# Second layer of a two-layer expert kernel: another order of the seven products, sums formed one step earlier, token operands in nine steps

## The chip, the core and the metric

The kernel runs on one core of a Trainium2 chip. A core has engines with a program each: TensorE (PE, matrix products), VectorE (DVE), ScalarE (ACT), GpSimd (POOL) and SyncE (SP, which here issues all transfers). PEld is PE's loading of weights. Engines wait for each other by semaphores. PE writes into PSUM, which has eight banks of 128 x 512 floats; all other tiles lie in SBUF. The metric is the device time of one execution in microseconds (us).

## The reference

```python
def reference(**kwargs):
    ...
    attn_out = _attn_ref(**attn_kwargs)      # attention in windows: B, H, S, D = 4, 8, 768, 64
    x = np.ascontiguousarray(attn_out.transpose(0, 2, 1, 3)).reshape(B * S, H * D)   # 3072 x 512
    x = _moe_ref(x=x, **moe_kwargs)
    return _moe2_ref(x=x, **moe2_kwargs)

def _moe_ref(x, w_gate, w_val, w_out):       # 512 -> 1536 -> 512
    gate = 1.0 / (1.0 + np.exp(-(x @ w_gate)))
    val = x @ w_val
    return (gate * val @ w_out).astype(np.float32)

def _moe2_ref(x, w_in, w_out):               # 512 -> 2048 -> 512
    h = x @ w_in
    g = h * (1.0 / (1.0 + np.exp(-h)))
    return (g @ w_out).astype(np.float32)
```

## The kernel before

Attention and the first layer (`_moe_ref`) come first; beside them `prepare2` makes the second layer's weights ready and puts them into DRAM. The change lies in the second layer (`_moe2_ref`), the last 500 us.

**Precision.** An operand is kept as two tiles, a high part and the rest. `split` (L79) makes them: a cast on ACT (L82), then a subtraction on DVE (L85). A product takes three matmuls for each 128 rows of depth: high x high, high x rest, rest x high.

**Seven products for eight.** The second layer works on blocks of 1024 tokens (b = 0, 1, 2). In a block each matrix is cut into 2 x 2 parts, and the 2 x 2 product is formed from seven products of sums of parts. Their names are A11, S1, S2, A12, S3, S4, A22. Three accumulators are used: A11 and then A12 go to c1; S1 and then S4 to c3; S2, then S3, then A22 to c2. After A11 c1 is copied to s1 (ACT); after S1 c3 is copied to s5 (ACT), and POOL adds s1 to it. After S2 DVE puts c2 + s1 into u2. The four parts of the result are c1 after A12 ("11"), c2 + s5 after S3 ("22"), c2 + s1 after A22 ("21") and c3 + u2 after S4 ("12").

**Stages.** A block has two stages. The first has eight *pairs* (`pair2`, p = 0 to 7), each of seven products of 6 matmuls, whose results go through Silu (ACT) into tiles g11, g12, g21, g22. `bank` hands out the eight PSUM banks in turn, three for a pair. After every second pair its `tail` is formed, in the next pair's code: DVE subtracts g11 from g12, and `form` splits the first operand of the output products. In the first pair of block 0, `fill` puts the first layer's last 12 matmuls (L90 to L94) between products.

The second stage is `out2`: 28 steps m = 0 to 27, seven products in the order of ORDER2 with four steps each. A step is two `unit`s (dp = 0, 1) of 6 matmuls. After unit m the call `form(b, m + AHEAD2)`, with AHEAD2 = 4, forms the operand `gf` of step m + 4: for S2, S3 and A22 first a sum of g tiles on DVE (`sub`, L630), and then the split. `gf` has four buffers, so the cast for step m + 4 writes where step m read. `done` takes up finished accumulators.

**The next block's tokens.** `x_parts` makes the seven operands xp of a block from the first layer's result y (two loads of 1 MB, `load_y`). It is a generator; each `next` runs it up to its next `yield`. For block 0 it is called in the last block of the first layer after f = 3, 4, ... 11; for the others from `beside(m)` in `out2`.

**Weights of the second layer** come in pieces (`next_granule`, tile `wr`) into a ring of five slots; two pieces serve a pair (the first A11, S2, S1, S3, the second the others), one serves two steps.

All orders are those of the program text: each engine works off its instructions in the order in which the code issues them.

Of the kernel before, what the change touches and what calls it, by code (L numbers as in the profile page):

```python
# [41 lines left out]
A11, S2, S1, S3, A12, A22, S4, A21 = range(8)  # L42
ORDER2 = (A11, S1, S2, A12, S3, S4, A22)
# [4 lines left out]
def moe_kernel(ctx: ExitStack, tc: tile.TileContext, qh, kh, vh, wg, wv, wo, w2i, w2o, out):  # L48
# [14 lines left out]
    def w_slot(i, name):  # L63

        return main.tile([P, 2, 2, 512], F32R, tag=f"w{i}", name=name)
# [13 lines left out]
    def split(hi, lo, src, lo_eng, hi_eng=nc.scalar):  # L79

        if hi_eng is nc.scalar:
            nc.scalar.copy(hi, src)  # L82
        else:
            hi_eng.tensor_copy(hi, src)
        lo_eng.tensor_tensor(out=lo, in0=src, in1=hi.bitcast(F32), op=ALU.subtract)  # L85
# [11 lines left out]
    class Unit:  # L97
# [29 lines left out]
        def part(self):  # L127
            self.u = self.slot(self.name)
            split(self.u[:, 0], self.u[:, 1], self.t, nc.gpsimd)
            if self.keep is not None:  # L130
                nc.sync.dma_start(out=self.keep, in_=self.u.bitcast(F32))
# [116 lines left out]
    def split_x(src, n, name, on_pool=0, hi_dve=()):  # L248
        xs = []
        for kt in range(KT):  # L250
            x = p1.tile([P, 2, 512], F32R, tag="x", name=f"{name}_{kt}", bufs=5)
            lo_eng = nc.gpsimd if kt >= KT - on_pool else nc.vector
            hi_eng = nc.vector if kt in hi_dve else nc.scalar
            split(x[:, 0, :n], x[:, 1, :n], src[:, kt, :n], lo_eng, hi_eng)
            xs.append(x)
        return xs
# [26 lines left out]
    with tc.manual_schedule():  # L283
# [29 lines left out]
        for t in range(1, n0):  # L313
            i = 5 + 2 * (t - 1)
# [96 lines left out]
        x = split_x(x32.pop(0), BLOCKS1[0], "x0", NP, NH)  # L411
# [7 lines left out]
        for bi in range(NB1 - 1):  # L419
            n = BLOCKS1[bi + 1] // P  # L420
            for jj in range(n):
                t = starts1[bi + 1] // P + jj
# [131 lines left out]
        def x_parts(b, ya, yb):  # L554

            b11, b21 = ya[:, 0:2], ya[:, 2:4]
            b12, b22 = yb[:, 0:2], yb[:, 2:4]
            t1 = w_slot(4, f"t1_{b}")[:, 0].bitcast(F32)

            def sub(o, i0, i1):  # L560
                nc.vector.tensor_tensor(out=o, in0=i0, in1=i1, op=ALU.subtract)

            def part(i, s):
                t = w_slot(i, f"xp{b}_{i}")
                split(t[:, 0], t[:, 1], s, nc.vector)
                xp[b].append(t)

            xp[b] = []
            part(0, b11)
            yield  # L570
            sub(t1, b12, b11)
            sub(b11, b22, t1)
            part(1, b11)
            yield
            part(2, t1)
            yield
            sub(b12, b22, b12)
            part(3, b12)
            yield
            part(4, b21)  # L580
            yield
            if b:

                tmp = p2.tile([P, 2, 2, 512], F32, tag="gf", name=f"xt{b}", bufs=AHEAD2)
                sub(tmp[:, 0], b21, b11)
                nc.scalar.copy(tmp[:, 1], b22)
                b21, b22 = tmp[:, 0], tmp[:, 1]
            else:
                sub(b21, b21, b11)
            part(5, b21)  # L590
            yield
            part(6, b22)
# [6 lines left out]
        def next_granule():  # L599
            n = loaded[0]  # L600
            loaded[0] += 1
            if n >= NB2 * NG:
                return
            w = w_slot(7 + n % NRING, f"wr{n}").rearrange("p a b c -> p (a b c)")
            k = n % NG
            if k < 2 * NPAIR:
                w = w.rearrange("p (a m c) -> p a m c", a=2, m=4)
                m = 4 - k % 2
                nc.sync.dma_start(out=w[:, :, :m].bitcast(F32), in_=w2i_d[k // 2, :, k % 2, :, :m])
            else:  # L610
                k -= 2 * NPAIR
                w = w.rearrange("p (b a m c) -> p b a m c", b=2, a=2, m=2)
                nc.sync.dma_start(out=w.bitcast(F32), in_=w2o_d[k // 2, k % 2])
            ring[n] = w
# [4 lines left out]
        def bank(name):  # L619
            turn[0] += 1  # L620
            return (ps_m, ps_a, ps_m, ps_a, ps_y, ps_y, ps_y, ps_y)[(turn[0] - 1) % 8](name)
# [4 lines left out]
        def add(o, a, b_):  # L626
            nc.vector.tensor_tensor(out=o, in0=a, in1=b_, op=ALU.add)  # L627

        def sub(o, a, b_):
            nc.vector.tensor_tensor(out=o, in0=a, in1=b_, op=ALU.subtract)  # L630

        def silu(o, i):
            nc.scalar.activation(out=o, in_=i, func=AF.Silu)  # L633

        g2 = {}

        def g2_of(b, p, r):
            pp = p // 2
            if (b, pp, r) not in g2:
                g2[b, pp, r] = p2.tile([P, 2, 512], F32, tag=f"g{pp}{r}", name=f"g{b}_{pp}_{r}")  # L640
            return g2[b, pp, r][:, p % 2]

        def pair2(b, p, fill, tail):

            n = f"{b}_{p}"
            k = b * NG + 2 * p
            c1, c2, c3 = bank(f"c1_{n}"), bank(f"c2_{n}"), bank(f"c3_{n}")
            X = xp[b]

            def prod(o, i, first):  # L650
                w = ring[k + i // 4]
                j = 0
                for kt in range(2):
                    for pw, px in ((0, 0), (0, 1), (1, 0)):
                        nc.tensor.matmul(  # L655
                            o,
                            w[:, pw, i % 4, kt * P : (kt + 1) * P],
                            X[i][:, px, kt],
                            start=first and j == 0,
                            stop=j == 5,  # L660
                            skip_group_check=not first,
                        )
                        j += 1
                if i in (S3, S4):
                    next_granule()

            s1, s5, u2 = t2(f"s1_{n}"), t2(f"s5_{n}"), t2(f"u2_{n}")
            prod(c1, A11, True)
            nc.scalar.copy(s1, c1)
            prod(c2, S2, True)  # L670
            add(u2, c2, s1)
            if tail:
                tail()
            prod(c3, S1, True)
            nc.scalar.copy(s5, c3)  # L675
            nc.gpsimd.tensor_tensor(out=s5, in0=s5, in1=s1, op=ALU.add)  # L676
            if fill:
                fill()
            prod(c2, S3, False)
            add(s5, c2, s5)  # L680
            silu(g2_of(b, p, "22"), s5)
            prod(c1, A12, False)
            silu(g2_of(b, p, "11"), c1)
            prod(c2, A22, False)
            add(s1, c2, s1)
            silu(g2_of(b, p, "21"), s1)
            prod(c3, S4, False)
            add(u2, c3, u2)
            silu(g2_of(b, p, "12"), u2)

            def tail_of():
                pp = p // 2
                if p % 2:

                    t = g2[b, pp, "12"]
                    sub(t, t, g2[b, pp, "11"])
                    form(b, pp)

            return tail_of

        gf = {}

        def form(b, m):

            if m >= 28:
                return
            i, pp = ORDER2[m // 4], m % 4
            t = {r: g2[b, pp, r] for r in ("11", "12", "21", "22")}
            if i == S2:
                sub(t["12"], t["22"], t["12"])  # L710
            elif i == S3:
                sub(t["11"], t["12"], t["11"])
            elif i == A22:
                sub(t["21"], t["21"], t["12"])
            src = t[{A11: "11", S1: "12", S2: "12", A12: "21", S3: "11", S4: "22", A22: "21"}[i]]
            f = p2.tile([P, 2, 2, 512], F32R, tag="gf", name=f"gf{b}_{m}", bufs=AHEAD2)
            split(f[:, 0], f[:, 1], src, nc.vector)
            gf[b, m] = f
# [75 lines left out]
        for bi, n in enumerate(BLOCKS1):  # L794
# [6 lines left out]
            for f in range(NF1):  # L801
# [20 lines left out]
                if f == NF1 - 1 and not last:  # L822
                    x = split_x(x32.pop(bi + 1), BLOCKS1[bi + 1], f"x{bi + 1}")
# [18 lines left out]
        for b in range(NB2):  # L842
            tail = None
            for p in range(NPAIR):
                fill = (lambda: emit_out1(*pending, t2)) if b == 0 and p == 0 else None
                tail = pair2(b, p, fill, tail)
            tail()

            def beside(m):
                nonlocal xgen  # L850
                if b + 1 == NB2:
                    return
                if m == 0:
                    xgen = x_parts(b + 1, *load_y(b + 1))
                if m in (8, 9, 10, 11, 16, 24, 25):
                    next(xgen, None)

            out2(b, beside)
# [72 lines left out]
```

## Time and profile before

| | |
|---|---|
| median of 3 runs | 1206.33 us (1205.33 to 1208.36) |
| profiled execution, its own time | 1207.34 us |
| its span, first to last instruction | 1205.6 us |
| busy: PE, DVE, ACT, POOL | 1155.8, 698.1, 484.2, 130.9 us |
| mean granted clock of PE | 0.989 of full speed |
| second layer, first matmul | at 701.44 us |

Times in rows count from the first instruction. The end of a matmul is modelled, so successive matmuls overlap in the records: their rate is read from starts, or from the length of a long merged row. Several like instructions in a row are merged ("x84"), and what the engine waited for stands in brackets, with the idle time before it.

### The profile page before, as it was taken

What the parts mean: (1) busy time and instruction counts of PE and PEld (TensorE: products, weight loads), DVE (VectorE), ACT (ScalarE), POOL (GpSimd) and SP (SyncE); (2) the same over time, 40 slices, a digit from 0 to 9 for tenths busy, and PEclk for the clock granted to TensorE, in tenths of its full rate; (3) what the DMA queues carried; (4) which work ended last, traced back from release to release, by engine and by line L of the source; (5) the groups of instructions that cost most, each with busy time, mean ns of one, the idle gap of its engine ahead of it and who ended that gap; (6) DMA issues with size and microseconds to landing.
All of it is one profiled execution on the core that took longest, in us unless ns stands there. A gap on an engine that the chain in (4) does not pass through costs nothing.

```text
span 1205.6 us, 16022 instructions
## 1 busy us (share of the span) xinstructions
PE 1155.8 (96%) x6319; PEld 929.8 (77%) x6319; DVE 698.1 (58%) x965; ACT 484.2 (40%) x708; POOL 130.9 (11%) x94
## 2 busy tenths in 40 slices
PE   8889899999999999999999999998999998999997
PEld 7667677888888788888878877786777786777886
DVE  7999965465455545554646424367733477543574
ACT  3554544344333434343423333344433444343441
POOL 2545520000000000000000001100011110011010
PEclk9899999999999999999999999998999998999999
DMA  9777766667665766665564545573665654655551
GB/s 313 236 237 238 245 225 245 201 213 241 195 208 192 231 223 202 233 222 184 183 236 131 202 157 179 187 279 111 238 203 181 261 200 165 220 183 189 189 206 62
DMA packets 79210, 248.51 MB, mean 206 GB/s; under 512 B 7584, under 2 KB 23968, under 8 KB 69920
## 3 DMA queue, kind: packets, MB, share of 16 engines
q1 hardware_dynamic: 79136, 247.49, 60.4%
q8 instruction: 50, 0.82, 0.3%
q14 instruction: 24, 0.20, 0.0%
HBM read 199.23 MB, written 48.23 MB: 205 GB/s over the span
## 4 chain that ended last, share of the span: by engine, by line
PE 49%; DVE 20%; issue 19%; DMA 6%; ACT 3%; POOL 3%; SPq 0%; DVEq 0%; POOLq 0%; ACTq 0%
PE pg L263 12%; PE pv L263 12%; PE o L763 8%; PE y L90 4%; PE y L92 4%; PE y L94 4%; POOL s L676 3%; DVE gf L85 3%; DVE g L630 2%; ACT gf L82 2%; PE c L655 2%; PE px L229 1%; DVE t_wg L122 1%; PE sc L189 1%; DVE t_wo L122 1%
## 5 line engine op out<-in xcount | busy, mean ns | idle before, releaser
L763 PE MATMUL o<-gf,wr 128*128 128x512 f32 x1008 | 240.4, 399 | 11.1 <-ACT gf L82 7.5
L655 PE MATMUL c<-xp,wr 128*128 128x512 f32 x1008 | 236.1, 392 | 10.9 <-DVE s L627 8.2
L763 PEld LDWEIGHTS o<-gf,wr 128*128 128x128 f32 x1008 | 193.5, 193 | 57.6 <-ACT gf L82 8.8
L655 PEld LDWEIGHTS c<-xp,wr 128*128 128x128 f32 x1008 | 187.3, 188 | 59.1 <-DVE s L627 19.2
L263 PE MATMUL pv<-x,w 128*128 128x512 f32 x864 | 215.9, 399 | 13.8 <-DVE sg L277 12.3
L263 PE MATMUL pg<-x,w 128*128 128x512 f32 x864 | 210.5, 392 | 1.4 <-POOL x L85 0.9
L263 PEld LDWEIGHTS pv<-x,w 128*128 128x128 f32 x864 | 162.8, 191 | 53.2 <-issue 14.7
L263 PEld LDWEIGHTS pg<-x,w 128*128 128x128 f32 x864 | 160.5, 188 | 37.5 <-POOL x L85 1.4
L85 DVE TENSOR_TENSOR gf<-g,gf 128x1024 fp32r<-128x1024 f32 x84 | 101.8, 1223 | 60.9 <-ACT gf L82 60.7
L676 POOL TENSOR_TENSOR s<-s,s 128x512 f32<-128x512 f32 x24 | 38.7, 1611 | 850.3 <-ACT s L675 833.1
L82 ACT CAST gf<-g 128x1024 fp32r<-128x1024 f32 x84 | 87.2, 1050 | 106.7 <-DVE g L630 89.9
L82 ACT CAST g<-sg 128x512 fp32r<-128x512 f32 x72 | 44.7, 621 | 156.9 <-DVE sg L277 156.9
L627 DVE TENSOR_TENSOR s<-c,s 128x512 f32<-128x512 f32 x48 | 33.2, 692 | 90.1 <-POOL s L676 47.3
L273 ACT ACTIVATE sg<-pg 128x512 f32<-128x512 f32 x72 | 42.9, 596 | 68.1 <-PE pg L263 54.9
L90 PE MATMUL y<-g,wor 128*128 128x512 f32 x240 | 66.3, 397 | 1.0 <-DVE y L532 1.0
L633 ACT ACTIVATE g<-s 128x512 f32<-128x512 f32 x48 | 30.3, 632 | 89.0 <-DVE s L627 89.0
L85 DVE TENSOR_TENSOR g<-sg,g 128x512 fp32r<-128x512 f32 x60 | 41.6, 693 | 41.8 <-ACT g L82 41.8
L92 PE MATMUL y<-g,wor 128*128 128x512 f32 x240 | 64.3, 390 | 0.0
L94 PE MATMUL y<-g,wor 128*128 128x512 f32 x240 | 64.2, 389 | 0.0
L630 DVE TENSOR_TENSOR g<-g,g 128x1024 f32<-128x1024 f32 x48 | 61.8, 1287 | 2.1 <-ACT g L633 2.1
L277 DVE TENSOR_TENSOR sg<-pv,sg 128x512 f32<-128x512 f32 x72 | 49.3, 685 | 21.7 <-PE pv L263 21.7
L92 PEld LDWEIGHTS y<-g,wor 128*128 128x128 f32 x240 | 45.1, 188 | 9.6
(120 smaller groups left out, 1129.2 us busy)
## 6 DMA issues: line engine op xcount, KB each, us to landing
wr<-w2o_d SPq DMA_DIRECT2D x42, 1024.0 KB, 4.8
wor<-wo_d SPq DMA_DIRECT2D x60, 512.0 KB, 4.8
wr<-w2i_d SPq DMA_DIRECT2D x24, 1024.0 KB, 5.1
wr<-w2i_d SPq DMA_DIRECT2D x24, 768.0 KB, 4.5
w2o_d<-coo SPq DMA_DIRECT2D x56, 256.0 KB, 2.8
w2i_d<-coi SPq DMA_DIRECT2D x24, 512.0 KB, 3.0
qA<-in_qh_dram SPq DMA_DIRECT2D x21, 512.0 KB, 4.8
k<-in_kh_dram SPq DMA_DIRECT2D x21, 512.0 KB, 5.4
```

Of the source, the lines that this page charges most:

```text
L82: nc.scalar.copy(hi, src)
L85: lo_eng.tensor_tensor(out=lo, in0=src, in1=hi.bitcast(F32), op=ALU.subtract)
L90: nc.tensor.matmul(o, w_hi, x_hi, start=first, stop=False)
L92: nc.tensor.matmul(o, w_hi, x_lo, start=False, stop=False)
L94: nc.tensor.matmul(o, w_lo, x_hi, start=False, stop=last)
L263: nc.tensor.matmul(o[:, :n], w[:, pw, kt * P : (kt + 1) * P], x[kt][:, px, :n], start=i == 0, stop=i == len(steps) - 1,)
L273: nc.scalar.activation(out=sg[:, :n], in_=psg[:, :n], func=AF.Sigmoid)
L277: nc.vector.tensor_tensor(out=sg[:, :n], in0=psv[:, :n], in1=sg[:, :n], op=ALU.mult)
L630: nc.vector.tensor_tensor(out=o, in0=a, in1=b_, op=ALU.subtract)
L655: nc.tensor.matmul(o, w[:, pw, i % 4, kt * P : (kt + 1) * P], X[i][:, px, kt], start=first and j == 0, stop=j == 5, skip_group_check=not f ...
L676: nc.gpsimd.tensor_tensor(out=s5, in0=s5, in1=s1, op=ALU.add)
L763: nc.tensor.matmul(c[at[i], dp], w[:, pw, pl, dp * P : (dp + 1) * P], f[:, px, pl], start=i in (A11, S1, S2) and pp == 0 and j == 0, stop= ...
```

## The change

Three edits, all in the second layer.

1. *Order of the products in a pair.* Before: A11, S2, (tail), S1, (fill), S3, A12, A22, S4. Now: A11, (tail), S1, (fill), S2, A12, S3, S4, A22, the order that `out2` has. The next weight pieces are asked for after S3 and A22 instead of S3 and S4.
2. *Sums in `form`.* The sum of step m + 1 is now issued in front of the split of step m, in `form_sum`.
3. *`x_parts` in nine pieces* instead of seven, called at m = 4, 9, 10, 11, 16, 17, 24, 25, 26 instead of 8, 9, 10, 11, 16, 24, 25.

```diff
             part(0, b11)
             yield
             sub(t1, b12, b11)
+            yield
             sub(b11, b22, t1)
+            yield
             part(1, b11)
+            sub(b12, b22, b12)
             yield
             part(2, t1)
             yield
-            sub(b12, b22, b12)
             part(3, b12)
-            yield
-            part(4, b21)
             yield
             if b:
 
                 tmp = p2.tile([P, 2, 2, 512], F32, tag="gf", name=f"xt{b}", bufs=AHEAD2)
                 sub(tmp[:, 0], b21, b11)
                 nc.scalar.copy(tmp[:, 1], b22)
+                part(4, b21)
                 b21, b22 = tmp[:, 0], tmp[:, 1]
             else:
+                part(4, b21)
                 sub(b21, b21, b11)
+            yield
             part(5, b21)
...
-                if i in (S3, S4):
+                if i in (S3, A22):
                     next_granule()
...
             prod(c1, A11, True)
             nc.scalar.copy(s1, c1)
-            prod(c2, S2, True)
-            add(u2, c2, s1)
             if tail:
                 tail()
             prod(c3, S1, True)
...
             if fill:
                 fill()
+            prod(c2, S2, True)
+            add(u2, c2, s1)
+            prod(c1, A12, False)
+            silu(g2_of(b, p, "11"), c1)
             prod(c2, S3, False)
             add(s5, c2, s5)
             silu(g2_of(b, p, "22"), s5)
-            prod(c1, A12, False)
-            silu(g2_of(b, p, "11"), c1)
+            prod(c3, S4, False)
+            add(u2, c3, u2)
+            silu(g2_of(b, p, "12"), u2)
             prod(c2, A22, False)
             add(s1, c2, s1)
             silu(g2_of(b, p, "21"), s1)
-            prod(c3, S4, False)
-            add(u2, c3, u2)
-            silu(g2_of(b, p, "12"), u2)
...
-        def form(b, m):
+        def form_sum(b, m):
 
             if m >= 28:
                 return
             i, pp = ORDER2[m // 4], m % 4
-            t = {r: g2[b, pp, r] for r in ("11", "12", "21", "22")}
-            if i == S2:
-                sub(t["12"], t["22"], t["12"])
-            elif i == S3:
-                sub(t["11"], t["12"], t["11"])
-            elif i == A22:
-                sub(t["21"], t["21"], t["12"])
-            src = t[{A11: "11", S1: "12", S2: "12", A12: "21", S3: "11", S4: "22", A22: "21"}[i]]
+            if i in (S2, S3, A22):
+                o, x, y = {S2: ("12", "22", "12"), S3: ("11", "12", "11"), A22: ("21", "21", "12")}[i]
+                sub(g2[b, pp, o], g2[b, pp, x], g2[b, pp, y])
+
+        def form(b, m):
+
+            form_sum(b, m + 1)
+            if m >= 28:
+                return
+            i, pp = ORDER2[m // 4], m % 4
+            r = {A11: "11", S1: "12", S2: "12", A12: "21", S3: "11", S4: "22", A22: "21"}[i]
+            src = g2[b, pp, r]
             f = p2.tile([P, 2, 2, 512], F32R, tag="gf", name=f"gf{b}_{m}", bufs=AHEAD2)
             split(f[:, 0], f[:, 1], src, nc.vector)
...
-                if m in (8, 9, 10, 11, 16, 24, 25):
+                if m in (4, 9, 10, 11, 16, 17, 24, 25, 26):
                     next(xgen, None)
```

PE in pair 4 of block 0, before. In the accumulators' names the number of the pair (4) is followed by one of the tile: c1 is 6255, c2 6256, c3 6257. The xp operands tell the product (0 A11, 1 S2, 2 S1, 3 S3, 4 A12, 5 A22, 6 S4).

```order
L655 MATMUL c_0_4_6255<-xp_0_5526,wr_6117 128x512 x6
L655 MATMUL c_0_4_6256<-xp_1_5586,wr_6117 128x512 x6
L655 MATMUL c_0_4_6257<-xp_2_5643,wr_6117 128x512 x6
L655 MATMUL c_0_4_6256<-xp_3_5703,wr_6117 128x512 x6
L655 MATMUL c_0_4_6255<-xp_4_5761,wr_6159 128x512 x6
L655 MATMUL c_0_4_6256<-xp_5_5811,wr_6159 128x512 x6
L655 MATMUL c_0_4_6257<-xp_6_5860,wr_6159 128x512 x6
```

The same pair on PE, now:

```order
L658 MATMUL c_0_4_6255<-xp_0_5526,wr_6117 128x512 x6
L658 MATMUL c_0_4_6257<-xp_2_5755,wr_6117 128x512 x6
L658 MATMUL c_0_4_6256<-xp_1_5696,wr_6117 128x512 x6
L658 MATMUL c_0_4_6255<-xp_4_5853,wr_6167 128x512 x6
L658 MATMUL c_0_4_6256<-xp_3_5804,wr_6117 128x512 x6
L658 MATMUL c_0_4_6257<-xp_6_5956,wr_6167 128x512 x6
L658 MATMUL c_0_4_6256<-xp_5_5901,wr_6167 128x512 x6
```

Between S1 (operand xp_2) and A22 (xp_5) stood S3 and A12; now four products stand there. In both orders one product stands between two uses of c2.

DVE from the end of pair 1 to the end of pair 2 of block 0, a pair with a tail, before (L627 adds, L630 is the tail's sum, L85 the second half of its split):

```order
L627 TENSOR_TENSOR u_0_1_6063<-c_0_1_6060,u_0_1_6063 128x512
L627 TENSOR_TENSOR u_0_2_6126<-c_0_2_6122,s_0_2_6124 128x512
L630 TENSOR_TENSOR g_0_12_6056<-g_0_12_6056,g_0_11_6036 128x1024
L85 TENSOR_TENSOR gf_0_6142<-g_0_11_6036,gf_0_6142 128x1024
L627 TENSOR_TENSOR s_0_2_6125<-c_0_2_6122,s_0_2_6125 128x512
L627 TENSOR_TENSOR s_0_2_6124<-c_0_2_6122,s_0_2_6124 128x512
L627 TENSOR_TENSOR u_0_2_6126<-c_0_2_6123,u_0_2_6126 128x512
```

And now (L630 adds, L633 is the sum):

```order
L630 TENSOR_TENSOR s_0_1_6061<-c_0_1_6059,s_0_1_6061 128x512
L633 TENSOR_TENSOR g_0_12_6045<-g_0_12_6045,g_0_11_6025 128x1024
L85 TENSOR_TENSOR gf_0_6135<-g_0_11_6025,gf_0_6135 128x1024
L630 TENSOR_TENSOR u_0_2_6126<-c_0_2_6122,s_0_2_6124 128x512
L630 TENSOR_TENSOR s_0_2_6125<-c_0_2_6122,s_0_2_6125 128x512
L630 TENSOR_TENSOR u_0_2_6126<-c_0_2_6123,u_0_2_6126 128x512
L630 TENSOR_TENSOR s_0_2_6124<-c_0_2_6122,s_0_2_6124 128x512
```

The tail's two instructions stood behind the add to u2 (u_0_2 from c_0_2_6122, c2) and now stand ahead of it.

DVE in `out2` of block 0, steps m = 9 to 13, before (gf_13 is formed at m = 9, gf_17 at m = 13; L561 are the sums of `x_parts`; y_0 and y_1 are the two loads, t_1 its t1):

```order
L85 TENSOR_TENSOR gf_13_6710<-g_1_21_6179,gf_13_6710 128x1024
L561 TENSOR_TENSOR t_1_6694<-y_1_6550,y_0_6548 128x1024
L561 TENSOR_TENSOR y_0_6548<-y_1_6550,t_1_6694 128x1024
L85 TENSOR_TENSOR xp_1_6717<-y_0_6548,xp_1_6717 128x1024
...
L85 TENSOR_TENSOR gf_15_6754<-g_3_21_6447,gf_15_6754 128x1024
L561 TENSOR_TENSOR y_1_6550<-y_1_6550 128x1024
L85 TENSOR_TENSOR xp_3_6760<-y_1_6550,xp_3_6760 128x1024
L630 TENSOR_TENSOR g_0_11_6036<-g_0_12_6056,g_0_11_6036 128x1024
L85 TENSOR_TENSOR gf_16_6776<-g_0_11_6036,gf_16_6776 128x1024
L630 TENSOR_TENSOR g_1_11_6170<-g_1_12_6190,g_1_11_6170 128x1024
L85 TENSOR_TENSOR gf_17_6792<-g_1_11_6170,gf_17_6792 128x1024
```

And now, from step m = 10 on (u2o are the adds of `done` after S2):

```order
L561 TENSOR_TENSOR y_0_6548<-y_1_6550,t_1_6622 128x1024
L630 TENSOR_TENSOR u2o_0_6738<-o_0_0_6531,s1o_0_6590 128x512
L630 TENSOR_TENSOR u2o_1_6746<-o_0_1_6532,s1o_1_6598 128x512
L633 TENSOR_TENSOR g_0_11_6025<-g_0_12_6045,g_0_11_6025 128x1024
L85 TENSOR_TENSOR gf_15_6749<-g_3_21_6458,gf_15_6749 128x1024
L85 TENSOR_TENSOR xp_1_6754<-y_0_6548,xp_1_6754 128x1024
L561 TENSOR_TENSOR y_1_6550<-y_1_6550 128x1024
L633 TENSOR_TENSOR g_1_11_6159<-g_1_12_6179,g_1_11_6159 128x1024
L85 TENSOR_TENSOR gf_16_6771<-g_0_11_6025,gf_16_6771 128x1024
L633 TENSOR_TENSOR g_2_11_6293<-g_2_12_6313,g_2_11_6293 128x1024
L85 TENSOR_TENSOR gf_17_6787<-g_1_11_6159,gf_17_6787 128x1024
```

A sum on a g tile was followed by the split of that tile; now a split of another operand stands between, and the sum belongs to the next step.

## Rows read from the trace of the kernel before

**Rows 1.** The page: busy time of each engine, its share of the span.

```profile
PE 1155.8 (96%) x6319; PEld 929.8 (77%) x6319; DVE 698.1 (58%) x965; ACT 484.2 (40%) x708; POOL 130.9 (11%) x94
```

**Rows 2.** All waits of PE from 701 us: total, times, longest.

```profile
PE c L655 <- DVE s L627: 8.2, 9, 0.9
PE o L763 <- ACT gf L82: 7.5, 3, 3.0
PE o L763 <- DVE gf L85: 3.4, 7, 0.8
PE c L655 <- DVE u L627: 1.4, 1, 1.4
```

**Rows 3.** Timeline of PE, start of `out2` of block 0: start, length, count.

```profile
787.01 0.39 PE L655 MATMUL c<-xp,wr 128*128 128x512 f32 x1
787.24 38.02 PE L763 MATMUL o<-gf,wr 128*128 128x512 f32 x167
```

**Rows 4.** Windows by stage: pairs and `out2` of block 0; pairs 1; `out2` 2.

```profile
core 0: us, PE busy (x) PEld busy (x) DVE busy (x) ACT busy (x) POOL busy (x), PEclk, DMA share, GB/s
701.44:787.24 85.80, 81.25 (x350) 64.70 (x349) 29.45 (x39) 32.69 (x53) 12.89 (x8) 1.00 0.55 186
787.24:872.40 85.16, 80.79 (x337) 64.61 (x336) 60.97 (x55) 36.71 (x41) 4.09 (x2) 0.96 0.56 206
872.40:954.09 81.69, 78.53 (x338) 62.44 (x336) 31.29 (x41) 30.96 (x51) 12.89 (x8) 1.00 0.58 197
...
1120.95:1201.79 80.84, 78.48 (x337) 63.94 (x335) 51.03 (x46) 29.62 (x33) 4.08 (x2) 0.98 0.42 153
```

**Rows 5.** Timeline of PE in `out2` of block 0, and the window behind it.

```profile
834.96 0.72 PE L763 MATMUL o<-gf,wr 128*128 128x512 f32 x1 [2.97 <-ACT gf L82]
...
836.90:841.60 4.70, 4.70 (x13) 3.64 (x12) 2.76 (x3) 1.69 (x2) 0.00 (x0) 0.50 0.00 0
```

**Rows 6.** Timeline of pairs 3 (no tail) and 4 (tail) of block 0.

```profile
741.01 1.29 POOL L676 TENSOR_TENSOR s<-s,s 128x512 f32<-128x512 f32 x1 [8.63 <-ACT s L675]
743.08 0.99 PEld L655 LDWEIGHTS c<-xp,wr 128*128 128x128 f32 x5 [0.53 <-DVE s L627]
...
748.92 0.69 DVE L627 TENSOR_TENSOR u<-c,s 128x512 f32<-128x512 f32 x1 [2.10 <-PE c L655]
749.53 1.22 DVE L630 TENSOR_TENSOR g<-g,g 128x1024 f32<-128x1024 f32 x1
...
750.66 1.22 DVE L85 TENSOR_TENSOR gf<-g,gf 128x1024 fp32r<-128x1024 f32 x1
750.88 2.15 POOL L676 TENSOR_TENSOR s<-s,s 128x512 f32<-128x512 f32 x1 [8.58 <-ACT s L675]
...
753.80 0.50 PE L655 MATMUL c<-xp,wr 128*128 128x512 f32 x1 [0.91 <-DVE s L627]
```

**Rows 7.** Timeline of the first pair of block 0.

```profile
708.43 0.59 ACT L669 COPY s<-c 128x512 f32<-128x512 f32 x1 [8.10 <-PE y L94]
...
709.80 1.43 PE L655 MATMUL c<-xp,wr 128*128 128x512 f32 x5 [1.40 <-DVE u L627]
```

**Rows 8.** Timeline of DVE and ACT in `out2` of block 0.

```profile
802.35 1.05 ACT L82 CAST gf<-g 128x1024 fp32r<-128x1024 f32 x1 [2.50 <-DVE g L630]
803.44 1.23 DVE L85 TENSOR_TENSOR gf<-g,gf 128x1024 fp32r<-128x1024 f32 x1 [1.20 <-ACT gf L82]
```

**Rows 9.** Timeline of PE near the end of block 2.

```profile
1192.06 0.49 PE L763 MATMUL o<-gf,wr 128*128 128x512 f32 x1 [1.59 <-ACT gf L82]
```

**Rows 10.** Tile y in `out2` of block 0: its two loads.

```profile
DMA to landing us min/median/max: 6.9/7.9/8.9
```

**Rows 11.** Timeline: DVE beside POOL, in `out2` and in the first layer.

```profile
811.69 2.32 DVE L630 TENSOR_TENSOR g<-g,g 128x1024 f32<-128x1024 f32 x1
...
108.07 1.80 POOL L85 TENSOR_TENSOR w<-t_wv,w 128x512 fp32r<-128x512 f32 x1 [3.44 <-ACT w L82]
108.66 0.68 DVE L277 TENSOR_TENSOR sg<-pv,sg 128x512 f32<-128x512 f32 x1
```

## Prediction

> **What bounds the kernel now.** I read the page first, then the waits of TensorE, then the six stages of the second layer one by one, then single waits in the timeline.
>
> The page has PE busy for 1155.8 us of a span of 1205.6 [rows 1]. A change that does not alter the matmuls can therefore only win back idle time, or time in which PE is slow. The waits say where the idle time of the second layer lies: 8.2 us of the pairs (L655) behind DVE's `s`, 7.5 and 3.4 us of the output products (L763) behind `gf` [rows 2].
>
> Those sums are too small a measure, so I look at whole stages. Without a wait PE starts a matmul every 0.2267 us: 167 of them fill 38.02 us, the last one counted with its full 0.39 [rows 3]. One product of a pair (6 matmuls) is 1.36 us, a step m of `out2` (12 matmuls) 2.72, a stage of 336 matmuls 76.2. The stages take 85.80 (with 12 matmuls of the first layer, so 78.9 would do), 81.69 twice, 85.16 twice (once for each of two blocks) and 80.84 [rows 4]. What they lose: 6.9 + 2 × 5.5 + 2 × 9.0 + 4.6 = 40.5 us. The listed waits are about half of it. The rest is waits too short to leave the modelled matmul records idle, and a slow clock: behind the 2.97 us wait at 834.96 PE runs at a granted clock of 0.50, the 1.2 GHz level, for some 4.7 us [rows 5], where a matmul takes twice its time. So a removed wait gives back more than its own length.
>
> **Part 1, the order in a pair.** Today bank c2 takes S2, then S3, then A22, and A22 is what waits. Before it DVE must add s5 to c2, and s5 comes from S1 over an ACT copy and a POOL addition. Between S1's end and A22 lie S3 and A12, 2.72 us, and in them copy, addition and add have to follow one another. In a pair without a tail POOL takes 1.29 us and the weight load of A22 is held 0.53 us. In a pair with a tail POOL takes 2.15, because DVE's split is running when it starts, and PE stands 0.91 [rows 6]. That repeats in all 24 pairs.
>
> In the new order S1 comes second and S3 fifth. s5 is needed at the end of S3, three products (4.1 us) after S1. Its chain is 0.59 [rows 7] + 1.29 or 2.15 [rows 6], with 0.3 after S1's last matmul 2.2 to 3.0 us. It is done before S3 ends. This wait goes in both kinds of pairs.
>
> What is late next is the other use of c2: S2, then A12, then S3. DVE must add u2 within A12's 1.36 us. Today the A22 ahead of one such add starts at 743.08; 24 matmuls later, with 0.11 for a restart (a first matmul takes 0.50 instead of 0.39), S2 is issued by 748.63, and the add starts at 748.92 and takes 0.69 [rows 6]. So 0.3 + 0.69 of 1.36 are used; this spacing exists today (S2, S1, S3) and shows no wait. But now the tail's sum and split stand ahead of that add on DVE. From the start of the pair: `add s1` of the last pair ends at 1.0 (0.3 + 0.69); the sum g12 - g11 runs 1.0 to 2.2 (its input comes from S4, which now ends a product earlier, so it does not wait); ACT copies c1 from 1.66 and casts (1.05 [rows 8]) to about 3.2; the split's second half runs 3.2 to 4.4. S2 ends at 4.08, so the add could start at 4.38; it starts at 4.4 and ends at 5.1. S3 is due at 5.44. It fits with 0.3 us.
>
> In the first pair of block 0 the first layer's last matmuls (L94) hold the ACT copy until 708.43 and thereby u2 and S3, 1.40 us [rows 7]. They now come before S2: the copy moves ahead by 1.36 us with them and ends at 707.66, A12 needs c1 at 701.44 + 30 × 0.2267 = 708.24, and u2 no longer waits for it. Gone too. The weight pieces are fetched one product later (after S3) and one is needed one product earlier; five ring slots are 2.5 pairs, about 24 us, against a landing time near 5, so I cost that at nothing. Sum of part 1: 6.9 + 5.5 + 5.5 = 17.9.
>
> **Part 2, sums one step ahead.** Today a step with a sum is a chain on one operand: sum on DVE, cast on ACT, split on DVE. ACT's cast takes 1.05 and idles 2.50 before it for the sum, so such a step takes 3.55, and DVE then idles 1.20 for the cast [rows 8]. PE uses a step in 2.72. So each of the 12 steps with a sum loses 0.83, and AHEAD2 = 4 gives 8.2 us from the end of unit m to the start of unit m + 4. In the last block the chains of A22 plus u2's adds end late, and PE stands 1.59 at 1192.06 [rows 9]. With the sum of m + 5 issued ahead of the split of m + 4, DVE has the sum to do while ACT casts. A step costs DVE 1.22 + 1.22 = 2.45 [rows 6], under 2.72. At the end of block 2: unit 23 ends 65.3 us into the stage, u2's second add ends at 66.2, the cast of 27 at 66.6, its split at 67.9; unit 27 is due at 65.3 + 3 × 1.36 = 69.4. The 4.6 go, but for 0.2 of the last matmul itself.
>
> **Part 3, nine steps for the tokens.** At m = 8 to 11 `x_parts` adds four splits and three sums to DVE today, of 1.22 us each. The new list of DVE work, in units of 1.22: step 3: two; 4: three; 5, 6: two; 7, 8: one; 9, 10: two; 11: u2's two adds and four; 12 to 14: two; 15: one; 16, 17: two; 18: one; 19: two and s5's adds; 20 to 23: two. The hard place is 11. DVE leaves step 10 at 33.8 us of the stage (unit 10 ends 29.9, cast 31.3, split 32.5, sum 33.8). Then 1.3 for the adds and six operations up to the split of 16: 42.4. Unit 16 is due at 16 × 2.72 = 43.5. Margin 1.1 us, or 1.8 if queued operations start 1.13 apart, as 749.53 and 750.66 do [rows 6]. Behind it the backlog shrinks. The first tokens' part moves from m = 8 to 4 and needs y: issued at the start of the stage, landed 6.9 to 8.9 us later [rows 10], wanted at 13.6. Parts 4 to 6 move to m = 24 to 26; they are worked off by about 75.5 us, and the next block wants them from 80 on. In the last block of the first layer two more steps fall to f = 10 and 11, where ACT and DVE have room and nothing of the first layer is read later. Sum of parts 2 and 3: 9.0 + 9.0 + 4.4 = 22.4.
>
> **DVE against POOL.** The new place of `add u2` lies under POOL's s5 addition in every pair, and two rows disagree on what that costs. A DVE sum of two SBUF tiles beside POOL takes 2.32 instead of 1.22; L277, with one operand in PSUM as `add u2` has, takes 0.68 beside a POOL operation of 1.80 [rows 11]. By the first the add is 1.1 longer, and the sum is smaller by the second rival's 20 us; by the second row it costs nothing. I take the second, the nearer in operands. The Trainium skill, "SBUF — State Buffer", section "Who interferes with whom", says that a VectorE instruction contends with GpSimd's reads when both its inputs lie in SBUF, and not with at most one there. By that rule the two rows don't disagree, and the sum would stay as it is.
>
> **The sum.** 17.9 + 22.4 = 40.3. I keep 1.8 back, an allowance of 0.3 us for each of six stages for a short wait that I do not see: 38.5. The profiled execution took 1207.34, so 1168.8; the median of the runs is 1206.33, 1.0 below it, which would give 1167.8. Forecast 1169.
>
> **The rivals.**
> - *The backlog at step 11 is not worked off.* Against it stands a margin of 1.1 to 1.8; for it, that this margin rests on eight operations in a row. If each costs 0.3 more, PE waits again at unit 16, and a wait of 2 to 3 us brings the 0.50 clock with it. At most both blocks keep their 9.0: 1168.8 + 18 = 1187.
> - *c2 still comes back after one product.* The old order also never used one bank twice running, so spacing alone proves nothing. If `add u2` is held as the 2.32 row was, 1.1 longer, it ends at 6.2, and S3 is 0.75 late, with 0.1 for the restart, in 24 pairs: 20 us, 1189. It decides once the add is more than 0.3 late.
> - *No change.* The time returns as another wait, on weights or DVE. Weights: no wait of PE for a transfer of `wr` is listed in the second layer [rows 2], and DVE is busy 61 of 85 us in `out2` [rows 4], 80% of 76. Then 1206.
> - *Slower: y comes late for m = 4.* ACT would block on the first cast and every form behind it. The loads are issued 0.6 into the stage, so ACT blocks once the first takes over 13.0 us instead of 6.9, and PE stops 5.8 later (8.2 less a form's 2.4), from 18.8 on. To undo the gain it would have to take 38 us in both blocks; at 42 it would be 1168.8 + 2 × 23 = 1215. Nothing in the rows is near that.
>
> **How the numbers follow.** Forecast 0.70, with its own range of 1165 to 1174 (the whole 40.5 off the median, or twelve more short waits of 0.4); backlog 0.13; c2 0.09; no change 0.04; slower 0.04. The first three are all faster by over 0.3%, which is about what a measurement of this kernel can tell from no change: 0.92. The range reaches from 1165 to 1182, which takes in the partial cases of the two rivals between 1174 and 1189.
>
> **What would show it.** After: PE waits in the second layer of at most a few us in sum; stages of 76 to 77 us (79 for the first); a granted clock of 0.99 or more in each; POOL no longer what DVE's `s` waits for; ACT's casts of `gf` no longer waiting for the sums on `g`. A wait of PE for DVE's `u` at S3 shows the c2 rival; a wait for `gf` around m = 15 to 17 shows the backlog; an ACT wait for the transfer of y shows the slower case. The prediction is wrong if DVE operations cost more in their new company, or if a dependency that the trace of before cannot show ties the early sums to something late.

## The result and the profile after

The changed kernel takes 1165.73 us (median of 4 runs, 1165.24 to 1166.24) against 1206.82 for the kernel before (median of 4 runs; the prediction knew three of them, 1206.33): ratio 0.9659, 95% interval 0.9643 to 0.9676, 41.1 us less. 1169 was forecast, with a range of 1165 to 1182. The profiled execution took 1165.85 us, with a span of 1164.1.

The page after, against [rows 1]. PE has the same 6319 matmuls and is busy for 17.6 us less; the matmuls of the second layer alone for 18.4 us less (the four lines further down), since fewer of them ran at the slow clock or behind a restart:

```profile
span 1164.1 us, 16020 instructions
...
PE 1138.2 (98%) x6319; PEld 927.7 (80%) x6319; DVE 695.6 (60%) x965; ACT 487.4 (42%) x708; POOL 124.5 (11%) x94
```

The costliest groups after (line, engine, operation, tiles; busy time, mean ns; idle before). The first two lines are all matmuls of the second layer, and the number at the end is the idle time ahead of them. Under them stand the same two groups before, in the same view for 701 to 1206 us, with 22.0 us of idle time and a longer mean matmul:

```profile
L658 PE MATMUL c<-xp,wr 128*128 128x512 f32 x1008 | 229.1, 389 | 0.0
L771 PE MATMUL o<-gf,wr 128*128 128x512 f32 x1008 | 229.0, 389 | 0.0
...
L763 PE MATMUL o<-gf,wr 128*128 128x512 f32 x1008 | 240.4, 399 | 11.1 <-ACT gf L82 7.5 <-DVE gf L85 3.4
L655 PE MATMUL c<-xp,wr 128*128 128x512 f32 x1008 | 236.1, 392 | 10.9 <-DVE s L627 8.2 <-DVE u L627 1.4
```

The timeline of PE over the second layer after, in which [rows 3, 7, 9] would stand. Each stage is one unbroken row (the first one from the end of the first layer's last matmuls on):

```profile
705.91 73.60 PE L658 MATMUL c<-xp,wr 128*128 128x512 f32 x324
779.35 76.32 PE L771 MATMUL o<-gf,wr 128*128 128x512 f32 x336
855.51 76.32 PE L658 MATMUL c<-xp,wr 128*128 128x512 f32 x336
931.67 76.32 PE L771 MATMUL o<-gf,wr 128*128 128x512 f32 x336
1007.83 76.32 PE L658 MATMUL c<-xp,wr 128*128 128x512 f32 x336
1083.99 76.32 PE L771 MATMUL o<-gf,wr 128*128 128x512 f32 x336
```

The windows by stage after, against [rows 4] (the same four stages; the last numbers are the granted clock, the transfers' share and GB/s):

```profile
700.47:779.35 78.88, 78.88 (x349) 65.32 (x348) 30.64 (x40) 33.22 (x53) 11.98 (x8) 1.00 0.57 194
779.35:855.51 76.16, 76.16 (x337) 63.06 (x336) 62.44 (x57) 37.76 (x41) 2.97 (x2) 1.00 0.66 243
855.51:931.67 76.16, 76.16 (x337) 63.06 (x336) 28.95 (x38) 31.06 (x50) 11.98 (x8) 1.00 0.59 199
...
1083.99:1160.31 76.32, 76.32 (x337) 62.88 (x335) 50.15 (x46) 30.17 (x33) 2.73 (x2) 1.00 0.47 171
```

The six stages lasted 500.4 us together and now last 459.8, so 40.5 us came out of them. PE is never idle in them, and the granted clock is 1.00 in each, against 0.96 to 1.00. The second layer also starts 0.97 us earlier (700.47 for 701.44). That is not the change: a matmul at 625.28 us of the kernel before already stood 0.97 us earlier after, ahead of the first instruction that the change moves (a sum of `x_parts` at 646.9 us before, 652.4 after). In the runs below the second layer starts between 700.6 and 701.7 us, whatever was edited, so a median can hold about 1 us that is not the edit's; the lengths of the stages don't.

### The profile page after: what moved, and what is told of

The parts are those of the page before. It is cut to its first block, busy times and chain, and to the rows that moved or that the text cites. A ratio compares the mean times of both kernels' runs of the same rounds, so it can differ in the third digit from the quotient of the medians.

```text
span 1164.1 us, 16020 instructions
## 1 busy us (share of the span) xinstructions
PE 1138.2 (98%) x6319; PEld 927.7 (80%) x6319; DVE 695.6 (60%) x965; ACT 487.4 (42%) x708; POOL 124.5 (11%) x94
## 4 chain that ended last, share of the span: by engine, by line
PE 83%; DVE 12%; DMA 3%; issue 1%; ACT 0%; SPq 0%; DVEq 0%; ACTq 0%
PE o L771 20%; PE c L658 20%; PE pv L263 13%; PE pg L263 13%; PE y L90 5%; PE y L92 5%; PE y L94 5%; PE sc L189 1%; PE px L229 1%; DVE t_wg L122 1%; DVE t_wo L122 1%; DVE t_wv L122 1%; DVE stg_wv L118 1%; DVE stg_wo L118 1%; DVE stg_wg L118 1%; DMA v<-in_vh_dram 1%
## 5 line engine op out<-in xcount | busy, mean ns | idle before, releaser
L658 PE MATMUL c<-xp,wr 128*128 128x512 f32 x1008 | 229.1, 389 | 0.0
L771 PE MATMUL o<-gf,wr 128*128 128x512 f32 x1008 | 229.0, 389 | 0.0
L771 PEld LDWEIGHTS o<-gf,wr 128*128 128x128 f32 x1008 | 189.2, 188 | 39.3
L85 DVE TENSOR_TENSOR gf<-g,gf 128x1024 fp32r<-128x1024 f32 x84 | 103.8, 1239 | 49.9 <-ACT gf L82 49.6
L678 POOL TENSOR_TENSOR s<-s,s 128x512 f32<-128x512 f32 x24 | 35.9, 1497 | 820.7 <-ACT s L677 820.7
L630 DVE TENSOR_TENSOR s<-c,s 128x512 f32<-128x512 f32 x48 | 33.2, 691 | 65.1 <-PE c L658 63.1
L85 DVE TENSOR_TENSOR g<-sg,g 128x512 fp32r<-128x512 f32 x60 | 41.5, 692 | 41.7 <-ACT g L82 41.7
L277 DVE TENSOR_TENSOR sg<-pv,sg 128x512 f32<-128x512 f32 x72 | 49.3, 684 | 21.3 <-PE pv L263 21.2
L633 DVE TENSOR_TENSOR g<-g,g 128x1024 f32<-128x1024 f32 x48 | 58.4, 1216 | 0.0
```

The source lines that it names most:

```text
L277: nc.vector.tensor_tensor(out=sg[:, :n], in0=psv[:, :n], in1=sg[:, :n], op=ALU.mult)
L658: nc.tensor.matmul(o, w[:, pw, i % 4, kt * P : (kt + 1) * P], X[i][:, px, kt], start=first and j == 0, stop=j == 5, skip_group_check=not f ...
L771: nc.tensor.matmul(c[at[i], dp], w[:, pw, pl, dp * P : (dp + 1) * P], f[:, px, pl], start=i in (A11, S1, S2) and pp == 0 and j == 0, stop= ...
```

## Experiments

Length of each stage in us, from its first matmul to the next stage's first (the last one to the end of its last matmul), in the profiled execution, and the median of all runs of that kernel; the three edits are 1 the order, 2 the sums ahead, 3 the tokens in nine steps:

```
kernel            pairs 0  out2 0  pairs 1  out2 1  pairs 2  out2 2   median
before              85.80   85.17    81.69   85.17    81.69   80.85  1206.82
after               78.88   76.16    76.16   76.16    76.16   76.32  1165.73
e1: edit 1          78.88   85.19    76.16   85.17    76.16   80.86  1187.80
e2: edit 2          85.81   80.14    81.69   78.60    81.68   76.32  1191.19
e3: edit 3          85.84   81.53    82.32   81.49    82.32   80.84  1200.07
e23: 2 and 3        85.83   76.16    81.71   76.16    81.69   76.32  1183.67
e12: 1 and 2        78.88   80.21    76.16   80.21    76.16   76.32  1173.62
e13: 1 and 3        78.88   81.50    76.16   81.52    76.16   80.83  1181.93
e4: s5 on DVE       82.79   85.15    78.38   85.18    78.42   79.28  1197.22
e5: S2, S3 in turn  87.97   76.16    85.24   76.16    85.24   76.32  1193.62
e6: 3 DVE ops       78.88   76.16    76.16   76.16    76.16   76.32  1166.43
e7: 12 DVE ops      78.88   81.18    76.16   81.16    76.16   76.32  1176.66
e8: y at m = 1      78.88   76.16    76.16   76.16    76.16   76.32  1166.51
```

**e1, the order alone.** The hunk of `pair2`, from `if i in (S3, A22)` to the last `silu`, and nothing else of the diff.

> The kernel before with edit 1 alone, the order of the products in a pair. Mine: the pairs' waits came from the chain S1, copy, POOL addition, add, and all 17.9 us of them go: pair stages of 78.9, 76.2, 76.2 us, out2 stages as before (85.2, 85.2, 80.8), 1188.9 us. Rival (c2 still comes back after one product, so the wait only changes its place): pair stages near 82, 1200 to 1206 us.

1187.80 us, ratio 0.9849 (0.9834 to 0.9864). The pair stages are those of after, `out2` is as before to 0.03 us. The two parts of the change don't touch each other here, and the pairs' share of 18 us is edit 1's alone.

**e4, is it the chain over POOL?** The kernel before, order unchanged; only

```diff
             nc.scalar.copy(s5, c3)
-            nc.gpsimd.tensor_tensor(out=s5, in0=s5, in1=s1, op=ALU.add)
+            add(s5, s5, s1)
```

> The kernel before, with the s5 addition of the pairs on DVE instead of POOL; order unchanged. Mine (the wait of A22 is the chain over POOL): pairs without a tail lose their wait; pairs with one keep about half, since the addition then stands behind the tail on DVE: 9 to 10 us gained, 1197. Rival (A22 waits because c2 comes back too soon, whatever computes s5): 1206.

1197.22 us, ratio 0.9925 (0.9910 to 0.9939). The pair stages fall by 3.0, 3.3 and 3.3 us. Of the waits of PE on DVE's `s`, 8.2 us in 9 waits [rows 2], this is left:

```profile
PE c L655 <- DVE s L627: 3.9, 9, 0.4
```

Nine waits of 0.4 instead of 0.9 are the nine pairs with a tail, as expected; those without a tail have lost theirs. The weight loads show that too: before they waited for `s` 23 times (19.2 us, the longest 1.3), and here nine times:

```profile
PEld c L655 <- DVE s L627: 7.7, 9, 0.9
```

c2 comes back after as few products as before, so it was the late s5 that PE waited for.

**e5, two products in one bank.** The changed kernel with two products exchanged:

```diff
             prod(c2, S2, True)
             add(u2, c2, s1)
-            prod(c1, A12, False)
-            silu(g2_of(b, p, "11"), c1)
             prod(c2, S3, False)
             add(s5, c2, s5)
             silu(g2_of(b, p, "22"), s5)
+            prod(c1, A12, False)
+            silu(g2_of(b, p, "11"), c1)
```

> The changed kernel, but A12 and S3 of the pairs exchanged, so that S2 and S3 follow each other in bank c2 (A11, S1, S2, S3, A12, S4, A22). Mine: S3 must wait until DVE has read S2's sum: 0.3 + 0.69 + 0.05, with 0.1 for the restart 1.15 us in each of 24 pairs, 27 us, 1193. Rival (one product between two uses of a bank was never needed, only s5 was late): 1166.

1193.62 us, ratio 0.9897 (0.9880 to 0.9913). Each pair stage is 9.1 us longer than after, 1.14 us a pair, against 1.15 expected. All 24 pairs wait:

```profile
PE c L658 <- DVE u L630: 20.0, 24, 0.9
```

So here a product between two uses of a bank is needed, and one of 1.36 us is enough. Neither the old nor the new order has two in turn; the rule is kept by the change, not introduced by it.

**e2, the sums ahead alone.** The hunks of `form_sum` and `form`, and nothing else.

> The kernel before with edit 2 alone, sums one step ahead. Mine: the last out2 falls to 76.4 (4.4 us); in blocks 0 and 1 the old places of the tokens' parts (m = 8 to 11) still leave DVE about 2.7 us late for unit 16, with up to 2.6 us of slow clock behind it, so 79 to 82 us; 11 to 17 us in all, 1190 to 1196. Rival (the tokens' parts are the whole cause in blocks 0 and 1): 1202. Rival (the sums are the whole cause): 1184.

1191.19 us, ratio 0.9875 (0.9860 to 0.9890). The last stage is 76.32 as in after; in blocks 0 and 1 one wait is left, of 2.08 us where 2.7 was expected, at the place that the walk of DVE's queue had given, unit 16 (193 matmuls stand ahead of it: 16 × 12 and the first of unit 16, which needs the cast alone):

```profile
787.42 43.95 PE L767 MATMUL o<-gf,wr 128*128 128x512 f32 x193
833.46 34.27 PE L767 MATMUL o<-gf,wr 128*128 128x512 f32 x143 [2.08 <-DVE gf L85]
...
995.29 32.73 PE L767 MATMUL o<-gf,wr 128*128 128x512 f32 x143 [2.08 <-DVE gf L85]
```

**e3, the nine steps alone.** The hunks of `x_parts` and of the list of m, and nothing else.

> The kernel before with edit 3 alone, the tokens in nine steps. Mine: the sums' chain of 3.55 us a step stays, PE loses 3 to 4 us around units 16 to 19 in small waits, without a slow clock: out2 of blocks 0 and 1 near 80, the last one as before (80.8); 10.5 us in all, 1196. Rival (the tokens' parts are the whole cause in blocks 0 and 1): 1189. Rival (without the sums it gains nothing): 1206.

1200.07 us, ratio 0.9949 (0.9934 to 0.9964); 1196 was expected. `out2` of blocks 0 and 1 loses 5.3 to 5.4 us instead of 3 to 4, in waits that are small one by one, and there is a loss that I had not expected, in the first pair of the next block:

```profile
834.28 3.02 PE L766 MATMUL o<-gf,wr 128*128 128x512 f32 x12 [0.54 <-DVE gf L85]
837.83 3.39 PE L766 MATMUL o<-gf,wr 128*128 128x512 f32 x12 [0.53 <-DVE gf L85]
841.99 21.82 PE L766 MATMUL o<-gf,wr 128*128 128x512 f32 x95 [0.77 <-DVE gf L85]
...
872.95 22.45 PE L658 MATMUL c<-xp,wr 128*128 128x512 f32 x96 [0.64 <-DVE u L630]
```

With the sums late, the moved parts 4 to 6 make DVE late for the next block's first `u2`, at 872.95, which costs pair stages 1 and 2 their 0.63 us; neither e2 (the parts at their old places) nor e23 (the sums ahead) has this loss. In e13, with the new order, the add comes as late (4.3 us after the start of the pairs, 4.2 in e3), but S1 and S2 now both stand ahead of it, and it costs nothing: the pair stages are 76.16.

**e23, e12, e13: the change less one edit each.** e23 is the changed kernel with the old `pair2`, e12 with the old `x_parts` and its list, e13 with the old `form`.

> Edits 2 and 3 without edit 1. Mine: out2 stages of 76.2 to 76.4, pair stages as before (85.8, 81.7, 81.7): 22.4 us, 1184.4. Rival (the pairs' order also shifts what out2 finds, for example later g tiles): out2 stages over 77 and 1187 or more.

> Edits 1 and 2 without edit 3 (tokens' parts in seven steps, at their old m). Mine: DVE is 2.7 us late for unit 16 of blocks 0 and 1, with up to 2.6 us of slow clock behind it: out2 stages of 79 to 82 there, 1171 to 1178 us. Rival (with the sums ahead, the old places do as well): 1166.

> Edits 1 and 3 without edit 2 (each sum directly in front of its own split). Mine: out2 loses 3 to 4 us in each of blocks 0 and 1 and 4.6 in the last: 1165.7 + 12 = 1178. Rival (the sums ahead matter only in the last block): 1170.

1183.67 us, ratio 0.9814 (0.9798 to 0.9830); 1173.62, 0.9730 (0.9713 to 0.9748); 1181.93, 0.9797 (0.9783 to 0.9812). Beside 1165.73, edit 1 is worth 17.9 us on top of the others, edit 2 16.2 and edit 3 7.9. By the stages, which leave out the first layer, it is 18.0, 15.2 and 8.1. Only e13 missed, by 4 us: `out2` again loses 5.3 to 5.4 us in blocks 0 and 1 where 3 to 4 was expected, and the second layer started 0.8 us later than in the profile after. Neither 2 nor 3 does alone what both do in `out2` of blocks 0 and 1: of 9.0 us lost per stage, edit 2 leaves 2.4 to 4.1, edit 3 leaves 5.3 to 5.4, both leave none. Edit 3 was tested as a whole: which of its moved calls are needed was not tried, but for the first one (e8).

**e6 and e7, how much slack is at step 11?** The changed kernel with 3, and with 12, added subtractions on DVE, into a tile that nobody reads:

```diff
                     next(xgen, None)
+                if m == 11:
+                    for _ in range(3):
+                        sub(spare, g2[b, 0, "22"][:, 0, :256], g2[b, 1, "22"][:, 0, :256])
```

> The changed kernel with 3 added DVE subtractions of 128x256 (1.2 us, into a tile nobody reads) in step m = 11 of blocks 0 and 1, ahead of the split for step 16. Mine: in the profile after, that split ends 1.9 us ahead of unit 16, so nothing is lost: 1165.7. Rival (the margin is used up by hand-overs): 1 to 2 us a block, 1168 to 1170.

> The same with 12 added subtractions (4.7 us). Mine: the split for step 16 is 2.8 us late, PE waits that long plus 0.1 and perhaps up to 2.6 us of slow clock in each of two blocks: 1171.5 to 1177. Rival (more slack than I count, since later steps catch up): 1166.

e6: 1166.43 us, 0.9667 (0.9654 to 0.9680), no wait of PE in the second layer, and every stage as long as after. e7: 1176.66, 0.9754 (0.9740 to 0.9767). The timeline of e7, DVE's added work and PE at unit 16:

```profile
819.28 5.48 DVE L633 TENSOR_TENSOR spare<-g,g 128x256 f32<-128x256 f32 x12
...
827.08 23.21 PE L771 MATMUL o<-gf,wr 128*128 128x512 f32 x94 [3.12 <-DVE gf L85]
```

5.4 us more work (the next operation starts at 824.67 instead of 819.28) gives 3.1 us of wait, so there were about 2 us of slack (the wait listed is a little shorter than the delay, because the last matmul's record reaches into it). The stage is 5.0 us longer, and its granted clock is 0.98 for 1.00, with 0.62 in the 4.5 us behind the wait: most of the rest is the slow clock there.

**e8, the slower rival's mechanism.** The changed kernel with the first tokens' part at m = 1:

```diff
-                if m in (4, 9, 10, 11, 16, 17, 24, 25, 26):
+                if m in (1, 9, 10, 11, 16, 17, 24, 25, 26):
```

> The changed kernel with the tokens' first part at m = 1 instead of 4. y lands 6.9 us or more after its issue and is wanted at about 5.7 us of the stage. Mine: ACT waits some 2 us for the transfer, but the forms have 5.8 us to spare, so PE does not wait: 1165.7. Rival (a late y stops PE, the slower case of the prediction): 2 us or more in two blocks, 1170.

1166.51 us, 0.9668 (0.9655 to 0.9681). ACT does wait for the transfer, twice, 1.6 us in sum, and PE never does. ACT's timeline in block 0:

```profile
787.76 1.05 ACT L82 CAST xp<-y 128x1024 fp32r<-128x1024 f32 x1 [0.74 <-DMA y<-yd]
```

And in the view of ACT's waits:

```profile
ACT xp L82 <- DMA y<-yd: 1.6, 2, 0.9
```

A late y is thus covered by the forms' lead, here for a wait of under 1 us each. A y so late that PE stops was not tried.

## Why the prediction held, step by step

**The size of what can be won.** The six stages against 336 matmuls at 0.2267 us gave 40.5 us; 40.5 came out. The listed waits alone, 20.5 us [rows 2], would have given half.

**Part 1** (17.9 us; e1 has 18.0 less in the pair stages). The new place of `add u2` behind the tail, after, in pair 4 of block 0, against [rows 6]:

```profile
742.08 1.22 DVE L633 TENSOR_TENSOR g<-g,g 128x1024 f32<-128x1024 f32 x1
744.45 1.23 DVE L85 TENSOR_TENSOR gf<-g,gf 128x1024 fp32r<-128x1024 f32 x1 [1.16 <-ACT gf L82]
744.98 1.84 POOL L678 TENSOR_TENSOR s<-s,s 128x512 f32<-128x512 f32 x1 [8.31 <-ACT s L677]
745.59 0.68 DVE L630 TENSOR_TENSOR u<-c,s 128x512 f32<-128x512 f32 x1
```

The pair starts at 700.47 + (12 + 4 × 42) × 0.2267 = 741.28. The add runs at 4.3 to 5.0 us of the pair, where 4.4 to 5.1 was worked out, and S3 is due at 5.44. It lies wholly beside POOL's addition and takes 0.68: the second of the two rows that disagreed, L277's [rows 11], was the right one. By the rule of the Trainium skill ("SBUF — State Buffer", section "Who interferes with whom") a VectorE instruction with at most one SBUF input does not contend with GpSimd outside its two-port modes, and `tensor_tensor` has no such mode. The trace agrees: the add takes 0.68 us here, and 0.68 to 0.69 in all 24 pairs. POOL itself still takes 1.84 where DVE's split is running; nobody waits for it now. In the first pair ACT's copy moved from 708.43 [rows 7] to 706.11, 2.32 us, of which 0.97 is the earlier start of the layer and 1.35 the move that was forecast as 1.36:

```profile
706.11 0.59 ACT L673 COPY s<-c 128x512 f32<-128x512 f32 x1 [5.79 <-PE y L94]
```

**Parts 2 and 3** (22.4 us; e23 has 22.5 less in the `out2` stages). The step that decided was the walk of DVE's queue at step 11. After, in block 0 (the stage starts at 779.35):

```profile
811.70 1.22 DVE L561 TENSOR_TENSOR y<-y,t 128x1024 f32<-128x1024 f32 x1
812.83 1.28 DVE L630 TENSOR_TENSOR u2o<-o,s1o 128x512 f32<-128x512 f32 x2
814.03 1.22 DVE L633 TENSOR_TENSOR g<-g,g 128x1024 f32<-128x1024 f32 x1
...
818.57 1.22 DVE L633 TENSOR_TENSOR g<-g,g 128x1024 f32<-128x1024 f32 x1
819.71 1.21 DVE L85 TENSOR_TENSOR gf<-g,gf 128x1024 fp32r<-128x1024 f32 x1
```

DVE leaves step 10 at 33.6 us of the stage (33.8 worked out), the split for 16 ends at 41.6, unit 16 is due at 43.5: 1.9 us of slack, against 1.1, or 1.8 with queued operations 1.13 apart. They do start that far apart. e6 and e7 give nearly the same number from the other side, about 2 us. Where ACT waited 89.9 us for the sums on `g` before (the first line, from a view of ACT's waits), it now waits mainly for PE, that is for the buffers:

```profile
ACT gf L82 <- DVE g L630: 89.9, 33, 4.2
...
ACT gf L82 <- PE o L771: 73.3, 49, 1.7
...
ACT gf L82 <- DVE g L633: 13.5, 7, 3.5
```

So one sign that the prediction named, casts of `gf` that no longer wait for the sums on `g`, came only in part. Six of the seven waits left are three in each of blocks 0 and 1 where DVE works off step 11 (in block 0 casts at 815.36, 819.90 and 822.17, behind 1.16, 3.48 and 1.22 us). They are the forecast backlog itself, and it stays 1.9 us short of PE.

At the end of block 2 the prediction had the split of 27 end at 67.9 us of the stage, with unit 27 due at 69.4. After, with the stage from 1083.99 on, it ends at 67.8:

```profile
1150.60 1.23 DVE L85 TENSOR_TENSOR gf<-g,gf 128x1024 fp32r<-128x1024 f32 x1 [0.30 <-ACT gf L82]
```

**What was off.** The forecast of 1168.8 stands against 1165.85 for the profiled execution. 1.8 of the 3.0 us is the allowance of 0.3 us a stage, which was not needed: no short wait was left. 1.0 is the first layer, as above, and that part is luck: nothing in the change moves it. The rest is 40.5 for 40.3. The measured median, 1165.73, lies close to the lower end of the range, 1165. One reading was a little off: at the 0.50 clock a matmul does not take quite twice its time. Behind the 2.97 us wait [rows 5] ten successive starts, from 836.82 to 840.65 us, are 0.427 us apart, 1.9 times 0.2267.

**The rivals.** The backlog at step 11 exists as a mechanism (e2, e7) but lies 1.9 us from doing harm. c2's return after one product is harmless, and would not be after none (e5). That a wait of 2 to 3 us brings the 0.50 clock with it, as the first rival has it, is true of some waits only (last section). Weights were never waited for, though `out2` now moves 243 GB/s for 206.

## What to carry to other kernels

Measure a stage by its number of matmuls times the interval of a stretch without waits, and not by the listed waits: here the stages had lost twice what was listed. For an engine that works in program order, walk its queue with durations from the trace up to the operation that another engine waits for, and compare with the due time; the slacks of 0.3 and of 1.1 to 1.8 us worked out in this way came out as 0.4 and 1.9. Splitting a chain (sum, cast, subtraction) over two steps and thinning out the work beside it paid together here: each alone left 2.4 to 5.4 of the 9.0 us of a stage.

## What had not been expected of the hardware

The same wait does not always bring the slow clock. In e2 both blocks have a wait of 2.08 us at the same matmul. The windows of 4.5 us behind them (granted clock in the third number from the end):

```profile
833.46:838.00 4.54, 4.54 (x13) 3.65 (x14) 4.49 (x4) 1.53 (x2) 0.00 (x0) 0.63 0.15 58
995.29:999.80 4.51, 4.51 (x20) 3.73 (x21) 4.49 (x4) 1.53 (x2) 0.00 (x0) 1.00 0.15 58
```

In the first most of the time ran at the 1.2 GHz level and 13 matmuls fit in, in the second all of it at 2.4 GHz and 20. The stages differ by 1.54 us (80.14 and 78.60), which is what the slow clock cost here; up to 2.6 had been expected. In e12 a wait of 2.07 us at that matmul was followed by a clock of 0.62 (826.09 to 830.60 us), and both its stages take 80.21. Likewise the wait of 1.59 us in the last stage of the kernel before [rows 9] stands in e4 too, but there the stage takes 79.28 instead of 80.85, with a clock of 1.00 for 0.98. What decides it no run here shows; about 1.5 us of such a comparison is not the edit's.
